# A written issue order in place of a list scheduler, in a kernel of windowed attention and a softplus MLP

## The chip, the core and the metric

One core of a Trainium2 chip runs the whole program. The metric is the device time of one execution in microseconds; the number for a kernel is the median of its runs. Five engines matter here: TensorE (PE, matrix products, with a separate row PEld for its weight loads), VectorE (DVE), ScalarE (ACT), GpSimd (POOL) and SyncE (SP, which here only issues DMA transfers). Each engine executes its own instructions strictly in the order in which the program lists them, and an instruction whose data is not there yet holds up everything behind it on that engine.

## The reference

Inputs are float32: q, k and v of shape (4, 8, 768, 64) and two weight matrices. Four sequences of 768 positions with 8 heads are attended, each row to 8 global keys and to the 96 nearest keys before it (the position itself included), with a bias that falls linearly with distance. The result, 3072 rows of 512, goes through an MLP with a softplus between its two products.

```python
scores = scale * np.matmul(q, k.transpose(0, 1, 3, 2))
is_global = pos[None, :] < int(n_global)          # 8
is_local = (rel >= 0) & (rel < int(n_local))      # 96
dist = np.where(is_global & ~is_local, float(n_local), np.abs(rel))
scores = scores + (-slopes[:, None, None] * dist[None, :, :])[None, :, :, :]
scores = np.where(is_global | is_local, scores, -1e9)
a = softmax(scores)                               # written out in the reference
x = (a @ v) as 3072 x 512
h = x @ w_in                                      # 512 x 2048
g = np.maximum(h, 0.0) + np.log1p(np.exp(-np.abs(h)))
out = g @ w_out                                   # 2048 x 512
```

## The kernel before

**Tiling.** The 3072 rows are 24 blocks of 128 positions. Two blocks of one sequence make a unit (`UNITS`, 12 of them), whose q, k and v are loaded together; blocks 2g and 2g+1 make group g of the MLP (12 groups). A block needs its own keys and those of the block before it, and the 8 global keys, which are copied into rows of the previous block that the window does not reach (`gk`, `gv`). Loads are float32 into a ring of 12 `raw` tiles; DVE, ACT or POOL casts them to bf16 (`cast`). Units 0 to 2 are transposed on PE (`tr`, evicted in two halves by `cp`), the others by DMA transposes on SP.

**Operations and their names.** The program is a list of 987 named operations, each one instruction or a few of one engine. In the order of the data they are:

- `ldq`, `ldk`, `ldv` with a unit's number, `win` and `wout` (eight 512 KB pieces of each weight matrix, line 831): loads, nearly all issued by SP. Units 0 to 2 load q and k in two halves, `.0` and `.1`.
- `castq`, `castk`, `castv` (lines 851 and 875), `cin`, `cout` (line 833): casts to bf16.
- `trq`, `trk` (lines 938 and 958), `cpq`, `cpk` (line 945): transposition of q and k, and its eviction.
- `biasFalse`, `biasTrue` (line 1311 to 1313): the bias of each head for the first block of a sequence and for the others. Blocks 0 and 1 get their bias through PE (`sb`, lines 1000 and 1044).
- `sc` (lines 1010 and 1063): the scores of a block, into the PSUM tiles `s_ps`; `z` (line 1089): DVE adds the bias; `ex` (lines 1023 and 1096): ACT takes the exponential.
- `pv` (line 1115): weights times values for half the heads, with a column of ones for the sum; `nm` (lines 1126 and 1127): DVE divides; `xt`: transposes the block's result, on PE for blocks 0 to 5 (line 1146, evicted by `xc`, line 1151), by DMA on SP for the others (line 1158).
- `a{g}.{p}` (line 1173): eight products with w_in for group g, pair p of 16 slices, into `h_ps[p % 2]`; `e` (line 1188) and `ln` (line 1199): softplus on ACT as ln(1 + exp(h)).
- `b{g}.{ns}.{x}` (line 1222): two or four products with w_out for half of group g; `oc` (line 1251) evicts 128 rows and `st` (line 1254) stores them.
- `fill0` to `fill34` (line 1335): matmuls on a blank tile that nothing reads.

PSUM is held in eight banks: `s_ps` twice two, `x_ps`, two `h_ps`, `o_ps`. Some products of the second layer use `s_ps` and `x_ps` too.

**What sets the order.** `Planner` is a list scheduler that runs while the program is built. Each operation carries the tiles that it reads and writes, an estimated duration and a rank; `due` moves the rank forward from the ranks of its users, plus a correction from the table `NUDGE` (some 280 entries), and `run` simulates the engines, gives each free engine its ready operation of lowest rank, and returns the order in which they started. The table `CHOICE` says on which engine an operation with a choice runs, where it departs from a default. The instructions are then emitted in that order:

```python
    pl.due(last, NUDGE)
    order = pl.run()
    ...
    for o in order:
        o.ins = o.fn()
```

A layer below adds semaphores for all data that crosses engines. DMA transfers take turns over eight semaphores, so that at most eight are in flight. Loads from unit 3 on also wait for a marked `a` operation (`gates`).

Of the kernel before, what the change touches and what calls it, by code (L numbers as in the profile page):

```python
# [16 lines left out]
class Op:  # L17
    __slots__ = (
        "eng", "dur", "lat", "rank", "fn", "deps", "users", "idx", "start", "end", "done",
        "left", "work", "pkt", "ins", "name", "sync", "count", "lane", "port", "alts",  # L20
    )


class Planner:

    LANES = 8
    COLD = 5.7
    FETCH = 18.0  # L30
    FETCH_COST = 1.0
    DMA_FIRST = 0.62
    DMA_LAST = 1.4
    LAT = {"PE": 0.30, "DVE": 0.15, "ACT": 0.21, "POOL": 0.15, "SP": 0.0}

    def __init__(self):
        self.ops = []
        self.writer = {}
        self.readers = {}

    def op(self, name, eng, dur, rank, fn, reads=(), writes=(), after=(), dma=None, sync=(), count=1,
           port=False, alts=None):
        o = Op()
        o.alts = None
        if alts:
            eng = CHOICE.get(name, eng)
            o.alts = [(e, d, e == "POOL" or (e == "DVE" and port)) for e, d in alts.items()]
            dur, port = next((d, p) for e, d, p in o.alts if e == eng)
            inner = fn
            fn = lambda: inner(eng)  # L50
        o.name, o.eng, o.dur, o.rank, o.fn = name, eng, dur, rank, fn
        o.idx = len(self.ops)
        o.lat = self.LAT[eng]
        o.work, o.pkt = dma if dma else (0.0, 0.0)
        o.start = o.end = o.ins = None
        o.sync = list(sync)
        o.count = count
        o.port = port or eng == "POOL"
        deps = set(after) | set(sync)
        for t in reads:  # L60
            if t in self.writer:
                deps.add(self.writer[t])
        for t in writes:
            if t in self.writer:
                deps.add(self.writer[t])
            deps.update(self.readers.get(t, ()))
        for t in reads:
            self.readers.setdefault(t, []).append(o)
        for t in writes:
            self.writer[t] = o  # L70
            self.readers[t] = []
        deps.discard(o)
        o.deps = deps
        self.ops.append(o)
        return o

    def due(self, last, shift, dma=2.4):

        users = {o: [] for o in self.ops}
        for o in self.ops:  # L80
            for d in o.deps:
                users[d].append(o)
        for o in reversed(self.ops):
            t = last(o)
            lag = o.dur + (o.work + dma if o.work else 0.0)
            for u in users[o]:
                t = min(t, u.rank - lag - (0.0 if u.eng == o.eng else o.lat))
            o.rank = t + shift.get(o.name, 0.0)

    def run(self, first=0.7, fixed=None, stretch=None):  # L90
        ops = self.ops
        dma_first, dma_last = self.DMA_FIRST, self.DMA_LAST
        stretch = stretch or (lambda o: 1.0)
        for o in ops:
            o.users = []
            o.done = False
            o.end = None
        for o in ops:
            o.left = len(o.deps)
            for d in o.deps:  # L100
                d.users.append(o)
        engines = ("PE", "DVE", "ACT", "POOL", "SP")
        ready = {e: [] for e in engines}
        free = {e: True for e in engines}
        events, seq = [], 0
        for o in ops:
            if not o.left:
                heapq.heappush(ready[o.eng], (o.rank, o.idx, o))
        now = first
        held = 0.0  # L110
        fetch = self.FETCH
        at = {e: 0 for e in engines}
        moved = [] if fixed is None else sorted((o for o in ops if o.work), key=lambda o: o.lane)
        queues = {"SP": [], "ACT": [], "POOL": []}
        order = []

        def push(t, kind, what):
            nonlocal seq
            seq += 1
            heapq.heappush(events, (t, seq, kind, what))  # L120

        def tell(users):
            for u in users:
                u.left -= 1
                if not u.left:
                    heapq.heappush(ready[u.eng], (u.rank, u.idx, u))

        def rates():
            live = [q for q in queues if queues[q] and queues[q][0][2] <= now + 1e-9]
            total = sum(queues[q][0][0].pkt for q in live)  # L130
            return {q: queues[q][0][0].pkt / total for q in live}

        while True:
            for e in engines:
                if free[e] and ready[e]:
                    if fixed is None:
                        o = ready[e][0][2]
                        if o.work:
                            if len(moved) >= self.LANES and not moved[-self.LANES].done:
                                continue  # L140
                            o.lane = len(moved)
                            moved.append(o)
                        heapq.heappop(ready[e])
                    else:
                        o = fixed[e][at[e]] if at[e] < len(fixed[e]) else None
                        if o is None or o.left:
                            continue
                        if o.work and o.lane >= self.LANES and not moved[o.lane - self.LANES].done:
                            continue
                        at[e] += 1  # L150
                    o.start = now
                    free[e] = False
                    order.append(o)
                    dur = o.dur * stretch(o)
                    if e == "PE" and now < self.COLD:
                        dur *= 2.0
                    if o.port:
                        dur += max(0.0, held - now)
                        held = now + dur
                    push(now + dur, "free", o)  # L160
            r = rates()
            t_dma, q_dma = None, None
            for q in queues:
                if not queues[q]:
                    continue
                if q in r:
                    t = now + queues[q][0][1] / r[q]
                else:
                    t = queues[q][0][2]
                if t_dma is None or t < t_dma:  # L170
                    t_dma, q_dma = t, q
            t_ev = events[0][0] if events else None
            if t_ev is None and t_dma is None:
                break
            t = min(x for x in (t_ev, t_dma) if x is not None)
            for q in r:
                queues[q][0][1] -= (t - now) * r[q]
            now = t
            if now >= fetch and r:
                queues[min(r)][0][1] += self.FETCH_COST  # L180
                fetch = 1e9
            for q in r:
                if queues[q][0][1] <= 1e-7:
                    o = queues[q].pop(0)[0]
                    o.end = now + dma_last
                    push(o.end, "done", o)
            while events and events[0][0] <= now + 1e-9:
                _, _, kind, o = heapq.heappop(events)
                if kind == "free":
                    free[o.eng] = True  # L190
                    if o.work:
                        queues[o.eng].append([o, o.work * stretch(o), now + dma_first + 1.8 * (o.eng == "POOL")])
                    else:
                        o.end = now
                        tell([u for u in o.users if u.eng == o.eng])
                        push(now + o.lat, "done", o)
                else:
                    o.done = True
                    tell([u for u in o.users if o.work or u.eng != o.eng])
        assert all(o.done for o in ops), [o.name for o in ops if not o.done][:20]  # L200
        self.span = max(o.end for o in ops)
        return order

# [61 lines left out]
NUDGE = {  # L265
    "a0.0": -1.75,
    "a0.1": 2,
    "a0.2": 8,
    "a0.3": -34.25,
    "a0.4": -1.25,  # L270
    "a0.5": -23.75,
    "a0.6": 1.75,
    "a1.1": 1,
    "a1.4": -9,
# [366 lines left out]
def kernel(  # L641
# [819 lines left out]
    if globals().get("PLAN_ONLY"):  # L1461
        return
# [42 lines left out]
```

## Time and profile before

| | us |
|---|---|
| median of 3 runs | 218.51 (217.66 to 218.69) |
| profiled execution, first to last instruction | 216.6 |
| PE busy | 208.8 |
| ACT busy | 166.6 |
| DVE busy | 116.0 |
| POOL busy | 78.8 |

The profile is of one execution; its own time is the span of 216.6 us plus what lies around it, and the median of the runs is 1.9 us above that span. It is read from several views. The page has the busy time of each engine and the chain of work that ended last: from the last instruction back, at each step to what released it. The chain can also be listed piece by piece for a stretch of time. The table of stretches gives busy time by engine for stretches of time that one chooses. The list of waits says which engine stood still for whose result. The timeline lists instructions in order of time. Rows give the time from the start, the duration, the engine, the line, the operation and what it writes and reads, as `out<-in`; a number after x counts instructions. Since each operation is a known number of instructions on its engine and each engine keeps its order, every instruction of the trace can be put to its operation by counting, and times of named operations in this text come from that.

### The profile page before, as it was taken

The page shows a single profiled execution, that of the slowest core. Times are in us where ns is not written, and L with a number is a line of the kernel's source. Part 1 is how long each engine was busy: PE and PEld are TensorE (multiplying, and loading weights), DVE is VectorE, ACT ScalarE, POOL GpSimd, SP SyncE. Part 2 cuts the span into 40 slices and gives each one's busy share as a digit, 9 for nine tenths or more (in the row PEclk, how much of TensorE's full clock was granted, in tenths as well). Part 3 has the DMA queues.
Part 4 walks back from the last instruction along what each step waited for, and adds up shares of the span by engine and source line. Part 5 has one row for each costly group of instructions (what it writes and reads, how often), then busy time and mean ns, then how long its engine had stood idle before and what let it go on. Part 6 is the DMA issues. An engine that isn't in the chain of part 4 may idle for free.

```text
span 216.6 us, 4949 instructions
## 1 busy us (share of the span) xinstructions
PE 208.8 (96%) x1974; PEld 142.4 (66%) x2003; DVE 116.0 (54%) x220; ACT 166.6 (77%) x227; POOL 78.8 (36%) x135
## 2 busy tenths in 40 slices
PE   7897999999999999999999999999999999999994
PEld 2455787657665787757767667756766767767554
DVE  7358977956489567337546546346645952101121
ACT  4798999996895699978788688678697878778300
POOL 4636624264159525900265462232237320000000
DMA  6999999999999499945886996892587212011112
GB/s 208 309 391 365 387 358 369 315 240 269 265 278 190 121 221 263 217 104 168 146 222 171 206 164 171 211 156 73 127 222 190 72 25 76 0 51 50 48 48 97
DMA packets 69846, 40.95 MB, mean 189 GB/s; under 512 B 30144, under 2 KB 61248, under 8 KB 69824
## 3 DMA queue, kind: packets, MB, share of 16 engines
q1 hardware_dynamic: 69392, 40.05, 71.1%
q10 hardware_dynamic: 432, 0.59, 0.9%
q8 instruction: 15, 0.25, 0.5%
q14 instruction: 7, 0.06, 0.1%
HBM read 27.26 MB, written 6.29 MB: 155 GB/s over the span
## 4 chain that ended last, share of the span: by engine, by line
PE 86%; DMA 6%; ACT 3%; DVE 2%; issue 1%; SPq 1%; ACTq 0%
PE h_ps L1173 37%; PE o_ps L1222 30%; PE s_ps L1222 6%; PE s_ps L1063 5%; PE x_ps L1115 5%; DMA raw<-in_k_dram 4%; DMA raw<-in_q_dram 2%; PE x_ps L1222 2%; ACT pb L1096 1%; ACT e L1188 1%; SPq L790 1%; PE s_ps L938 1%; ACT g L1199 0%; DVE vb L875 0%; DVE z L1089 0%
## 5 line engine op out<-in xcount | busy, mean ns | idle before, releaser
L1173 PE MATMUL h_ps<-XT,w_in_bf 128*128 128x256 bf16 x768 | 95.6, 273 | 0.2
L1173 PEld LDWEIGHTS <-w_in_bf 128*128 128x128 bf16 x768 | 73.1, 98 | 17.6 <-issue 0.6
L1188 ACT ACTIVATE e<-h_ps 128x512 f32<-128x512 f32 x96 | 60.1, 630 | 22.2 <-PE h_ps L1173 22.0
L1222 PE MATMUL o_ps<-w_out_bf,g 128*128 128x512 bf16 (+1 forms) x295 | 73.6, 371 | 1.2
L1222 PEld LDWEIGHTS <-g 128*128 128x128 bf16 x416 | 37.3, 98 | 28.9
L1089 DVE TENSOR_TENSOR z<-s_ps,biasA 128x1024 f32<-128x1024 f32 x38 | 45.8, 1218 | 15.0 <-PE s_ps L1063 9.2
L1199 ACT ACTIVATE g<-e 128x1024 bf16<-128x1024 f32 x48 | 50.5, 1056 | 1.3
L1096 ACT ACTIVATE pb<-z 128x1024 bf16<-128x1024 f32 (+1 forms) x44 | 43.4, 989 | 9.1 <-DVE z L1089 9.1
L1251 DVE COPY osb<-o_ps 128x512 f32<-128x512 f32 (+1 forms) x20 | 13.4, 671 | 38.2 <-PE o_ps L1222 37.9
L875 POOL CAST vb<-raw 64x512 bf16<-64x512 f32 x38 | 23.3, 614 | 15.7 <-DMA raw<-in_v_dram 14.4
L981 POOL COPY vb<-vb 4x512 bf16<-4x512 bf16 x27 | 16.5, 610 | 33.6 <-PE x_ps L1115 32.1
L875 POOL CAST kb<-raw 64x512 bf16<-64x512 f32 x32 | 19.6, 613 | 22.8 <-DMA raw<-in_k_dram 21.6
L1115 PEld LDWEIGHTS <-pb 128*128 128x128 bf16 x352 | 16.3, 98 | 7.3 <-ACT pb L1096 1.0
L1127 DVE TENSOR_TENSOR xs<-x_ps,rcp 128x256 bf16<-128x256 f32 x40 | 17.0, 424 | 1.6 <-DVE rcp L1126 0.3
L1126 DVE RECIPROCAL rcp<-x_ps 128x4 f32<-128x4 f32 x40 | 7.2, 179 | 17.7 <-PE x_ps L1115 17.3
L1115 PE MATMUL x_ps<-vb,pb 128*128 128x65 bf16 x304 | 15.8, 193 | 0.0
L1222 PE MATMUL s_ps<-w_out_bf,g 128*128 128x512 bf16 (+1 forms) x62 | 13.0, 352 | 0.1
L1335 PE MATMUL x_ps<-blank 128*128 128x512 bf16 x33 | 11.0, 484 | 1.4 <-DVE blank L1274 1.2
L1063 PEld LDWEIGHTS <-kT 64*128 64x128 bf16 x224 | 6.8, 94 | 5.1 <-issue 5.1
L1063 PE MATMUL s_ps<-qT,kT 64*128 64x128 bf16 x224 | 9.9, 218 | 0.1
L1089 DVE TENSOR_TENSOR z<-s_ps,bias 128x512 f32<-128x512 f32 x6 | 3.9, 686 | 7.0 <-PE s_ps L1063 6.9
L1335 PEld LDWEIGHTS <-blank 128*128 128x128 bf16 x35 | 3.7, 117 | 5.9 <-issue 3.3
(82 smaller groups left out, 109.0 us busy)
## 6 DMA issues: line engine op xcount, KB each, us to landing
raw<-in_v_dram SPq DMA_DIRECT2D x12, 512.0 KB, 5.5
out_dram<-osb SPq DMA_DIRECT2D x23, 256.0 KB, 2.3
raw<-in_q_dram SPq DMA_DIRECT2D x9, 512.0 KB, 4.5
raw<-in_k_dram SPq DMA_DIRECT2D x9, 512.0 KB, 4.8
raw<-in_moe_w_in_dram SPq DMA_DIRECT2D x8, 512.0 KB, 9.1
raw<-in_moe_w_out_dram SPq DMA_DIRECT2D x8, 512.0 KB, 8.9
raw<-in_k_dram SPq DMA_DIRECT2D x6, 256.0 KB, 8.2
raw<-in_q_dram SPq DMA_DIRECT2D x4, 256.0 KB, 7.1
```

Source lines behind the costliest of these rows:

```text
L875: copy_on[eng](dst, src)
L981: copy_on[eng](vb_of(prev)[sl, :, 0:D], vb_of(first)[sl, :, 0:D])
L1063: nc.tensor.matmul(reg if unit_of(n) in WIDE else reg.rearrange("p (r t) -> p r t", r=2), kt[rows, 2 * part + m, :], qv(rows, 2 * part + m ...
L1089: nc.vector.tensor_tensor(z, src, bias, ALU.add)
L1096: nc.scalar.activation(pb[:, 0:nr, :].rearrange("p (y a) b -> p y (a b)", y=2), src, AF.Exp, scale=1.0 / root_d)
L1115: nc.tensor.matmul(xv[:, h, :], pb[:, 4 * (h % 2) + 2 * part + h // 2 if lone else u_all * (2 * (h % 2) + h // 2) + u, :], vb_of(prev if u ...
L1127: nc.vector.tensor_tensor(xs[:, 4 * part : 4 * part + 4, :], xv[:, :, 0:D], rcp[:][:, :, None].to_broadcast([P, 4, D]), ALU.mult,)
L1173: last = nc.tensor.matmul(hv[:, j, :], w_in_bf[:, m, fb * P : fb * P + P], XT[g % NXG][:, m, :], start=(m == 0), stop=(m == NM - 1),)
L1188: nc.scalar.activation(e[:, p % 2, :, :].rearrange("p j (b t r) -> p (j b) r t", b=2, r=2), hb[:].rearrange("p (a r t) -> p a r t", a=4, r=2),
L1199: nc.scalar.activation(gt[:, 2 * p - 2 : 2 * p + 2, :].rearrange("p a t -> p (a t)"), e[:].rearrange("p a j t -> p (a j t)"), AF.Ln, bias=1.0,
L1222: nc.tensor.matmul(bank(key)[:, 0 : z - a], gt[:, fb, ns * P : ns * P + P], w_out_bf[:, fb, a:z], start=(fb == 0), stop=(fb == NFB - 1),)
L1335: nc.tensor.matmul(x_ps[:], blank[:, 0:P], blank[:])
```

## The change

The scheduler, its ranks, `NUDGE` and `CHOICE` are gone. `ORDER` is a string that lists all 987 operations with a letter for the engine (P, V, A, G, S for PE, DVE, ACT, POOL, SP), and the instructions are emitted in the order of that list. It was found by a search over whole orders, in which a PSUM tile is read by one engine at a time. The 987 operations and what each computes stay the same; `in_order` asserts that each stands behind what it depends on. 125 operations run on another engine than before: 39 go from POOL to DVE, 29 from POOL to ACT, 25 from DVE to ACT, 14 from DVE to POOL, 10 from ACT to DVE and 8 from ACT to POOL. Many, and all kinds, stand at another place. The diff, with the parts of the list that the text speaks of:

```diff
-class Planner:
-...
+class Program:
+    def __init__(self, placed):
+        self.placed = placed
+        self.ops, self.writer, self.readers = {}, {}, {}
+
     def op(self, name, eng, dur, rank, fn, reads=(), writes=(), after=(), dma=None, sync=(), count=1,
-           port=False, alts=None):
+           port=False, alts=None, mutex=None):
         o = Op()
-...
+        o.name, o.eng, o.fn, o.sync, o.ins = name, eng, fn, list(sync), None
         if alts:
-            eng = CHOICE.get(name, eng)
-...
+            o.eng = self.placed[name]
+            assert o.eng in alts, (name, o.eng)
+            o.fn = lambda: fn(o.eng)
+        assert o.eng == self.placed[name], name
         deps = set(after) | set(sync)
...
+    def in_order(self):
+        done = set()
+        for name in self.placed:
+            o = self.ops[name]
+            assert all(d.name in done for d in o.deps), (name, [d.name for d in o.deps if d.name not in done])
+            done.add(name)
+            yield o
+        assert len(done) == len(self.ops)
+
+ENGINES = {"P": "PE", "V": "DVE", "A": "ACT", "G": "POOL", "S": "SP"}
+ORDER = """
+blank:V table:A ones:G ldk0.0:S ldq0.0:A ident:G fill0:P ldk0.1:S ldq0.1:A fill1:P iota:G fill2:P ldv0:S fill3:P
+ldq1.1:S dl0a:V fill4:P dl1a:V ldk1.0:S dl0b:V fill5:P dl1c:V fill6:P ldk1.1:S dl0c:V fill7:P dl1e:V d0:G fill8:P
+castk0.0:A d0e:V ldv1:S fill9:P biasTrue0:V biasFalse7:A ldq1.0:S biasTrue5:V fill10:P biasTrue4:A biasTrue6:V
+biasFalse3:A fill11:P biasTrue1:A win1:S biasFalse6:V castq0.1:G biasFalse5:A fill12:P win3:S castq0.0:A castk0.1:G
+biasFalse1:A biasTrue3:A trq0.0:P biasFalse4:G biasTrue2:A trk0.0:P win0:S cpq0.0:A biasFalse0:G fill13:P fill14:P
+cpk0.0:A fill15:P win2:S castq1.1:V fill16:P biasFalse2:A fill17:P cpq0.1:V cpk0.1:A fill18:P castk1.0:G win4:S
+sb0.0:P biasTrue7:A castv0.10:V fill19:P castv0.00:G castv0.11:A sc0.0:P castk1.1:V sb1.1:P ex0.0:A sc1.1:P
+castv0.01:G ex0.1:A sb1.0:P sc1.0:P ex1.1:A fill20:P pv0.0:P fill21:P ex1.0:A fill22:P castv1.00:G nm0.0:V trk1.0:P
+fill23:P castq1.0:V pv0.1:P castv1.11:A fill24:P castv1.01:V pv1.1:P win5:S cpk1.0:A fill25:P nm0.1:V win7:S
+trq1.0:P cpk1.1:A cin1:G nm1.1:V win6:S fill26:P fill27:P cpq1.0:A xt0:P pv1.0:P cpq1.1:A fill28:P ldk2.1:S nm1.0:V
+castv1.10:A sc2.0:P ldk2.0:S xc0:A gv4.0:V fill29:P fill30:P z2.0:V xt1:P cin0:G fill31:P xc1:A z2.1:V sc3.0:P
+gv4.1:A fill32:P cin3:G a0.1:P z3.0:V ex2.0:A ex2.1:A pv2.0:P cin2:G a0.0:P ldq2.1:S e0.1:A nm2.0:V ldq2.0:S ex3.0:A
+gk4:G pv2.1:P sc3.1:P nm2.1:V a0.3:P e0.0:A cin4:G wout0:S z3.1:V ln0.0:A xt2:P a0.2:P cin5:G wout2:S e0.3:A xc2:V
+pv3.0:P e0.2:A fill33:P a0.5:P wout1:S cin7:V ex3.1:A nm3.0:V a0.4:P e0.5:A wout3:S cin6:V pv3.1:P fill34:P e0.4:A
+castk2.1:G nm3.1:V ldv2:S a0.7:P ln0.1:A castk2.0:G wout4:S a0.6:P castq2.1:V e0.7:A ln0.2:A xt3:P castq2.0:V
+trk2.0:P xc3:V trq2.0:P e0.6:A a1.1:P cout0:G cpq2.0:V cpk2.0:A cpk2.1:A a1.0:P cpq2.1:V e1.1:A wout5:S cout2:V
+...
+castk3.10:G ln1.2:A b0.0.10:P b0.1.8:P castk3.01:G b0.1.10:P e1.7:A cout7:G trk3:S pv5.1:P ln1.3:A
+...
+e11.4:A ln11.2:A b11.1.4:P b11.1.4.384:P a11.6:P e11.7:A b11.0.4:P e11.6:A ln11.3:A b11.1.8.384:P b10.1.8:P
+b10.1.12:P b11.0.8:P oc10.1.0:V b11.1.12.384:P b11.0.12:P st10.1.0:S oc11.1.384:A st11.1.384:S b11.1.8:P oc11.0.0:A
+b11.1.12:P b11.1.0.256:P st11.0.0:S b11.1.4.256:P oc11.1.0:V b11.1.8.256:P b11.1.12.256:P st11.1.0:S oc11.1.256:A
+st11.1.256:A
+"""
+PLACED = {w.rpartition(":")[0]: ENGINES[w.rpartition(":")[2]] for w in ORDER.split()}
...
-NUDGE = {
-    "a0.0": -1.75,
-...
-CHOICE = {
-    "biasFalse0": "DVE",
-...
-    pl = Planner()
+    pl = Program(PLACED)
...
-            op(f"cp{which}{i}.{r}", engs[r % len(engs)], 0.0, rank + 0.1 * r, ev, reads=held([key]), writes=outs,
+            op(f"cp{which}{i}.{r}", engs[r % len(engs)], 0.0, rank + 0.1 * r, ev, reads=held([key]), writes=outs, mutex=held([key])[0],
...
-    pl.due(last, NUDGE)
-    order = pl.run()
-...
-    for o in order:
+    for o in pl.in_order():
         o.ins = o.fn()
```

In the old order the loads of the head stood on SP as `ldk0.1 ldk0.0 ldq1.1 ldv0 ldq1.0 win0 ldk1.0 win1 win3 ldk1.1 win2 ldv1 win4 win5 win6 win7 ldk2.0 ldk2.1 ldq2.1 ldq2.0 wout1 wout2 wout0 ldv2 wout3 wout4 wout6 wout7 ldq3 ldk3 wout5 ldv3 ldq4 ldk4 trq3 ldv4 trk3`; in the new order the second half of that stretch is `wout0 wout2 wout1 wout3 ldv2 wout4 wout5 ldq3 ldk3 wout6 wout7 ldk4 ldv3 trq3 trk3 ldq4 ldv4`.

More of the change, by code (lines that the diff above doesn't have):

```diff
@@ L17 @@
 class Op:
[L18 to L21, printed above, removed]
[L24 to L39 removed]
+    __slots__ = ("name", "eng", "fn", "deps", "sync", "ins")
+class Program:
+    def __init__(self, placed):
+        self.placed = placed
+        self.ops, self.writer, self.readers = {}, {}, {}
     def op(self, name, eng, dur, rank, fn, reads=(), writes=(), after=(), dma=None, sync=(), count=1,
[L42 removed]
+           port=False, alts=None, mutex=None):
         o = Op()
[L44 removed]
+        o.name, o.eng, o.fn, o.sync, o.ins = name, eng, fn, list(sync), None
         if alts:
[L46 to L58 removed]
+            o.eng = self.placed[name]
+            assert o.eng in alts, (name, o.eng)
+            o.fn = lambda: fn(o.eng)
+        assert o.eng == self.placed[name], name
         deps = set(after) | set(sync)
@@ L90, in run @@
[L90 to L202, printed above, removed]
```

429 lines of the change are left out of this document (59 added, 370 removed).

## The prediction

> **What bounds the kernel now.** The page first: the busy row of each engine and the chain that ended last.
>
> ```profile
> span 216.6 us, 4949 instructions
> PE 208.8 (96%) x1974; PEld 142.4 (66%) x2003; DVE 116.0 (54%) x220; ACT 166.6 (77%) x227; POOL 78.8 (36%) x135
> PE 86%; DMA 6%; ACT 3%; DVE 2%; issue 1%; SPq 1%; ACTq 0%
> ```
>
> TensorE (PE) carries 86% of the chain, so a new order pays only where PE stands still or does nothing useful. The table of stretches says where that is (the stretch, its length, then busy time and instructions of PE, PE's weight loads, DVE, ACT and POOL, the granted clock, the DMA share and GB/s).
>
> ```profile
> 1.16:6.69 5.53, 5.52 (x14) 1.94 (x14) 4.04 (x17) 3.49 (x7) 2.91 (x8) 1.00 0.83 282
> 6.69:30.37 23.68, 21.55 (x253) 15.45 (x254) 15.98 (x34) 21.22 (x36) 12.35 (x17) 1.00 1.06 365
> 150.00:200.00 50.00, 49.65 (x457) 35.00 (x462) 19.68 (x35) 39.88 (x52) 10.41 (x19) 1.00 0.34 91
> 213.70:216.60 2.90, 0.00 (x0) 0.00 (x0) 0.29 (x1) 0.00 (x0) 0.00 (x0) 1.00 0.15 45
> ```
>
> I cut at 30.37 because there `a1.1` begins, the first piece of group 1, and both orders have done exactly the same PE work before it. That head has 2.13 us of idle PE and 21 fillers that compute nothing. From 30.37 to 213.70 the same view gives 181.77 us of PE in 183.33, and the table of waits names no engine and no transfer that PE waits for there: its five PE rows all lie in the head.
>
> ```profile
> PE x_ps L1335 <- DVE blank L1274: 1.2, 1, 1.2
> PE s_ps L1063 <- DVE kTa L945: 0.7, 1, 0.7
> PE h_ps L1010 <- DVE kTa L945: 0.7, 1, 0.7
> PE o_ps L1115 <- ACT pb L1096: 0.4, 1, 0.4
> PE x_ps L1335 <- issue: 0.2, 1, 0.2
> ```
>
> So after 30.37 there is nothing to win and all to lose. The chain inside the head says what holds it:
>
> ```profile
> 6.91 8.91 DMA raw<-in_k_dram
> 15.84 0.67 DVE kb L851
> 18.08 0.69 DVE kTa L945
> 19.13 0.84 DVE vb L875
> 20.00 0.70 DVE z L1089
> 20.79 0.63 ACT pb L1096
> 27.56 1.03 PE h_ps L1173 x8
> ```
>
> Unit 1's keys land at 15.81 and its values at 18.95, because w_in pieces were put between them. VectorE (DVE) can therefore add the first bias to block 2 only at 20.00, ScalarE (ACT) starts `ex2.0` at 20.79 and then runs without a stop until `e0.5` ends at 27.51, and only then comes `a0.7` on PE.
>
> **The head, step by step.** The DMA queue is full from 4 to 50 us (share about 1.06 above), so a load moved forward gains what the loads it passes weigh. Landing to landing in this execution: 0.67 us for a 256 KB half of q or k, 1.75 for v, 1.36 for a w_in or w_out piece; one w_in piece took 2.52.
> - First transposition. The new order has ACT cast the first key half (4.48, step 0.52), then three small and two wide biases (steps 0.21 and 0.32 from their rows, 1.27 together), then `castq0.0` (0.62): 6.89 instead of 6.54 for the last q half. `trq0.0` stands ahead of the seed `sb0.0` now and starts at 6.93; before, it came at 7.41. Thirteen fillers instead of fourteen stand ahead, so PE stops for about 0.3 us.
> - Block 0. Six fillers (0.217 each, from the 1.67 us of the seven at 8.41), the seed, one filler, then `sc0.0` at 10.1 to 10.5 (before 10.73). The bias multiply on POOL has no row of 128 columns; between the 0.29 of its 128 copy and the 0.95 of the 256 multiply it has 2.6 us of room before the seed, so it costs nothing.
> - Unit 1. The new SP order sends all of k1, v1 and q1 before any w_in: v1 lands near 11.3 (5.80 of the fourth half, 1.75, three of 0.67, 1.75; up to 12.4 if a slow piece lies ahead), q1 0.67 later, instead of 18.95 and 9.25. `trq1.0` runs at 14.4 to 14.8 and both ACT evictions behind it (0.48 a step) end at 16.0 to 16.6, so `sc2.0` comes at 16.1 to 16.75 instead of 18.82.
> - Group 0. w_in 0 now lands at 16.4 to 17.6 (the spread is the 1.15 by which one piece was slow) and is cast on POOL (1.04): `a0.1` at 18.0 to 18.7, before 19.16. `ex2.0` starts at 18.2 to 18.8 on ACT, not 20.79. From it to the end of `e0.5` both orders have the same ten ACT operations, which took 6.72: 24.9 to 25.5. The last w_in lands at 24.79, as before, since the same bytes lie ahead of it; its cast moves to DVE (0.68). So `a0.7` can start at 25.5 to 26.3, before 27.27.
> - End of the head. The last load of unit 2, q, lands at 27.50 in both (same bytes ahead). With its DVE cast (0.64), 0.09 of hand-over and the eight transposes `trq2.0` (0.50), `a1.1` cannot come before 28.7. PE's own work gives the same: 6.93 plus 21.55 busy plus one more filler 0.22 is 28.7. Between 28.7 and the old 30.37 I take 29.0, near the floor, because the ACT chain above has 0.5 to 1 us of room. Gain 1.4, bounds 1.7 and 0.
>
> **The body.** It holds the same 271 PE pieces. I took the step from each kind of piece to the next kind from the trace and counted the pairs in both orders: 182.9 us before, 182.8 after (score matmuls stand behind four-product w_out pieces six times instead of nine, where they cost 0.3 more than behind others). I take 0. 125 operations change engine: 68 leave POOL, ACT gets 54 and gives 18. Priced by their rows, ACT rises by 15 us to about 181 (84% of the new span), POOL falls by 25, DVE stays. The cover is PE: the densest stretch, group 3, has 10.0 us of ACT work under 11.0 of PE; in the old order group 0 had 10.5 under 10.7. A store eviction on ACT has no row at 512 columns; between 0.27 (128 columns) and the 0.63 of an exponential of that shape I take 0.6. PE-to-PE round trips after 30 us keep at least 0.3 us: the tightest is `e11.5`, 0.63 plus hand-over under the 1.09 of the two pieces between `a11.5` and `a11.7`. The DMA transposes of x for the second block of a group have 4.8 to 6.6 us from the end of its `pv` to the group's first piece; they need 0.75 for the division and 2.4 from issue to landing (`xt8`: 72.53 to 74.96). SP's queue stays in order: stores now stand between loads, and each waits for its copy. If they held a load by a microsecond, the rooms above take it. Cost 0, bound +1.
>
> **The tail.** Last piece, 128-column copy, 64 KB store, as before: ACT copies (0.27) and issues where DVE (0.29) and SP did. 0, within 0.1.
>
> Sum: 216.6 - 1.4 = 215.2 span. The median of the runs lies 1.9 above this execution's span, so 217.1.
>
> **A rule weighed.** The timeline of the start:
>
> ```profile
> 1.17 6.07 PE L1335 MATMUL x_ps<-blank 128*128 128x512 bf16 x14 [1.17 <-DVE blank L1274]
> 8.41 1.67 PE L1335 MATMUL x_ps<-blank 128*128 128x512 bf16 x7
> ```
>
> Fourteen fillers take 6.07 us (0.43 apart), seven later ones 1.67 (0.217 apart), at a granted clock of 1.00 throughout; PE had not stopped once before it sped up near 7 us. In the new order it stops for 0.3 us just then. The Trainium skill, TensorE: Matmul & The Clock Gate, "What's actually happening", says that half speed ends after one busy window of about 3.4 us and that the windows run free. The trace agrees in that the speed changes once, early. By that rule the stop could cost one more window at half speed, an estimate of 1.7 us by that page.
>
> **Rivals.**
> - Half speed lasts on. If the stop keeps PE at 0.43 us a filler up to the seed, two transpositions of 0.45 and six fillers of 0.217 take twice as long: 2.2 us, of which the stops that the head still has take up some 0.5. PE's own work already binds at 28.7, so `a1.1` comes at 30.4: no gain, 218.5. Against it: 0.3 us is small beside the 5.9 of unbroken work ahead of it. 0.2, in which hand-overs that I set too low end too.
> - Slower: unit 3's transposed keys are late. In POOL's new order `castk3.10` and `castk3.01` stand behind `cout6`, which waits for w_out 6, and SP has two loads and `trq3` ahead of `trk3`. `sc6.0` needs it, and comes at 51.2 (before 55.06, of which 3.5 is its new place). By the queue, `trk3` lands at 52.92 less the two loads it now passes (3.7): 49.2, 2.0 early. But if w_out 6 lands as late as the old last piece (44.14), cast 1.04 and two casts 0.61 end at 46.4; `trq3` held SP 3.35 and `trk3` took 4.7 from issue to landing: 54.5, PE stops 3.3 us, 220.4. It decides once `trk3` lands after 53.7. 0.18.
> - More gain. If no w_in piece is slow by 1.15, all landings move up by that and the floor is 27.6: 216.0. For it: all other pieces take 1.36. Against: PE's own 28.7. 0.08.
> - The order is the old one in writing: excluded, since the operations above move.
>
> **Numbers.** Main case 0.54 with its own range 216.6 to 217.7. A change of 0.5% (1.1 us) is about what a measurement tells, that is 217.4 and 219.6. Part of the main case lies above 217.4: faster 0.53, same 0.29, slower 0.18. The range takes the main case, the larger gain and no gain, and part of the slower case: 215.9 to 219.3.
>
> **What would show it.** Right: `ex2.0` near 18.5, `a1.1` near 29.0, no PE wait after that, ACT near 181 us, and PE ending 183.3 us after `a1.1`, near 212.3. Wrong: PE waits for kT, XT or e between 30 and 200 us; a filler spacing of 0.43 past 8 us; `a1.1` later than 30.

## The result

The new order takes 216.25 us (median of 6 runs, 216.09 to 216.60), the old one 218.53 beside it. The ratio is 0.9905, with a 95% interval of 0.9883 to 0.9928: 2.3 us faster, where 1.4 were forecast. The profiled execution has a span of 214.2 us and a time of 216.13.

The page of the new order, busy rows and shares of the chain that ended last:

```profile
span 214.2 us, 4986 instructions
PE 208.3 (97%) x2003; PEld 142.3 (66%) x2003; DVE 117.9 (55%) x230; ACT 179.1 (84%) x263; POOL 55.4 (26%) x89
PE 90%; DMA 7%; SPq 1%; ACT 1%; POOL 0%; issue 0%
```

ACT does 12.5 us more than before and POOL 23.4 less, and PE carries 90% of the chain instead of 86%. The table of stretches of the new order (stretch, length, busy time and instructions of PE, PE's weight loads, DVE, ACT and POOL, granted clock, DMA share, GB/s), in its own cuts for the head and the body and in two of the old ones:

```profile
1.16:6.69 5.53, 4.46 (x13) 1.58 (x13) 2.53 (x13) 3.42 (x10) 1.82 (x7) 1.00 0.80 262
...
6.69:28.36 21.67, 21.19 (x254) 15.41 (x255) 14.33 (x33) 20.90 (x36) 11.96 (x17) 1.00 1.07 377
28.36:212.30 183.94, 182.65 (x1740) 125.31 (x1737) 100.75 (x183) 154.39 (x219) 40.99 (x62) 1.00 0.70 170
...
150.00:200.00 50.00, 50.00 (x423) 32.89 (x422) 20.39 (x38) 38.77 (x54) 4.77 (x8) 1.00 0.31 78
```

`a1.1`, the end of the head, begins at 28.36 instead of 30.37. PE's waits in the new order, the whole list:

```profile
PE x_ps L933 <- DVE blank L872: 1.2, 1, 1.2
PE s_ps L536 <- POOL qb L449: 1.3, 1, 1.3
PE o_ps L713 <- ACT pb L694: 0.2, 1, 0.2
```

All three are in the head: the first filler, the first transposition and `pv2.0`. The chain of the new order through the head, in order of time (start, duration, what):

```profile
2.06 6.16 DMA raw<-in_v_dram
8.65 8.16 DMA raw<-in_moe_w_in_dram
16.86 1.05 POOL w_in_bf L431
17.91 0.61 ACT vb L579
18.55 0.64 ACT pb L694
...
27.68 0.89 PE s_ps L536 x16
28.58 1.53 PE h_ps L771 x14
```

No key or value of unit 1 is in it any more (the values in its first row are unit 0's). It runs over w_in 0 (landing at 16.81), ACT's `ex2.0` (18.55), and then PE without a gap. The step from the cast of w_in 0 to ACT's copy is the view's inference: ACT's piece before that copy ended at 17.88, so w_in 0 held `ex2.0` by 0.03 us at most. `a0.1`, at 17.95, needs both that cast, which ended at 17.90, and the copy `xc1`, which ended at 17.88. The timeline of the new order at both ends of the head:

```profile
1.17 4.46 PE L933 MATMUL x_ps<-blank 128*128 128x512 bf16 x13 [1.17 <-DVE blank L872]
6.89 0.62 PE L536 MATMUL s_ps<-ident,qb 128*128 128x128 bf16 x8 [1.25 <-POOL qb L449]
...
27.43 0.43 DVE L449 CAST qb<-raw 128x512 bf16<-128x512 f32 x1 [0.17 <-DMA raw<-in_q_dram]
27.97 0.61 PE L536 MATMUL s_ps<-ident,qb 128*128 128x128 bf16 x8
28.41 1.25 PE L771 MATMUL h_ps<-XT,w_in_bf 128*128 128x256 bf16 x10
```

The last cast of unit 2 follows its load (27.41) and ends at 27.86, just before the last transposition. PE has no pause in front of that transposition, though: its weight loads follow those of the one before at an unbroken 0.056 us from each to the next. So `a1.1` came when PE's own stream was through, and the load was in time by some 0.05 us.

**A ledger.** The records of PE's weight loads are complete in both traces (2003), unlike those of its matmuls, so a piece's place can be taken from its weight loads. From the first load of `a1.1` to the last load of the program the new order takes 182.38 us. In it every piece has one fixed price, the step between its matmuls and the next ones in the new order, whose matmul records are complete too: 0.87 for an `a` piece, 0.86 for a four-product w_out piece, 0.66 for 16 score matmuls (0.55, and 0.11 at the border before them), 0.24 for eight `pv`, 0.22 for four transposes of x, whatever stands beside it. What exceeds these prices is a stop, and the new order has none (0.01 us in all). A span is then `a1.1`, plus 182.38, plus stops, plus the rest behind the last weight load. All runs, worked out in this way from their traces (stops is the body less 182.38):

| kernel | median, us | ratio and 95% interval | span | `a1.1` | stops | rest |
|---|---|---|---|---|---|---|
| before | 218.53 | | 216.6 | 30.37 | 0.67 | 3.1 |
| new order | 216.25 | 0.9905 (0.9883 to 0.9928) | 214.2 | 28.36 | 0.00 | 3.5 |
| newhead_oldbody | 221.36 | 1.0139 (1.0107 to 1.0171) | 219.4 | 28.39 | 5.49 | 3.1 |
| newhead_oldbody2 | 217.24 | 0.9979 (0.9949 to 1.0008) | 215.4 | 28.15 | 1.73 | 3.1 |
| oldhead_newbody | 219.50 | 1.0065 (1.0037 to 1.0093) | 217.4 | 30.34 | 1.17 | 3.5 |
| new_oldloads | 226.67 | 1.0372 (1.0339 to 1.0406) | 225.3 | 39.45 | 0.00 | 3.5 |
| old_newloads | 224.57 | 1.0284 (1.0244 to 1.0324) | 222.0 | 35.19 | 1.34 | 3.1 |
| v1_late | 226.27 | 1.0383 (1.0336 to 1.0430) | 224.0 | 38.11 | 0.06 | 3.5 |
| no_late_fill | 217.18 | 0.9947 (0.9920 to 0.9973) | 215.3 | 28.24 | 1.15 | 3.5 |
| no_early_fill | 218.15 | 0.9993 (0.9968 to 1.0017) | 216.9 | 30.96 | 0.12 | 3.5 |
| two_readers | 219.20 | 1.0040 (1.0024 to 1.0056) | 217.3 | 30.42 | 1.02 | 3.5 |
| old_one_reader | 218.21 | 1.0002 (0.9981 to 1.0023) | 215.9 | 29.13 | 1.30 | 3.1 |
| end_sp | 215.81 | 0.9873 (0.9847 to 0.9899) | 213.7 | 28.28 | 0.00 | 3.0 |
| margins | 217.11 | 0.9927 (0.9900 to 0.9955) | 214.5 | 28.24 | 0.44 | 3.5 |

So the 2.33 us of span (216.55 to 214.22) came as 2.01 in the head and 0.67 in the body, less 0.35 behind the last load.

### The profile page after: what moved, and what is told of

Its sections match the earlier page's. It is cut to its first block, busy times and chain, and to the rows that moved or that the text cites. A ratio compares the mean times of both kernels' runs of the same rounds, so it can differ in the third digit from the quotient of the medians.

```text
span 214.2 us, 4986 instructions
## 1 busy us (share of the span) xinstructions
PE 208.3 (97%) x2003; PEld 142.3 (66%) x2003; DVE 117.9 (55%) x230; ACT 179.1 (84%) x263; POOL 55.4 (26%) x89
## 4 chain that ended last, share of the span: by engine, by line
PE 90%; DMA 7%; SPq 1%; ACT 1%; POOL 0%; issue 0%
PE h_ps L771 40%; PE o_ps L820 31%; PE s_ps L820 6%; PE s_ps L661 5%; PE x_ps L713 4%; DMA raw<-in_moe_w_in_dram 4%; DMA raw<-in_v_dram 3%; PE x_ps L820 2%; SPq L388 1%; POOL w_in_bf L431 0%; PE o_ps L713 0%; PE s_ps L536 0%; ACT pb L694 0%; ACT vb L579 0%; PE o_ps L744 0%; PE x_ps L744 0%
## 5 line engine op out<-in xcount | busy, mean ns | idle before, releaser
L820 PE MATMUL o_ps<-w_out_bf,g 128*128 128x512 bf16 (+1 forms) x320 | 76.8, 371 | 0.0
L786 ACT ACTIVATE e<-h_ps 128x512 f32<-128x512 f32 x96 | 59.3, 630 | 15.5 <-PE h_ps L771 14.9
L849 DVE COPY osb<-o_ps 128x512 f32<-128x512 f32 x13 | 9.0, 690 | 24.2 <-PE o_ps L820 24.1
L713 PEld LDWEIGHTS <-pb 128*128 128x128 bf16 x352 | 16.9, 98 | 6.1 <-ACT pb L694 0.5
L473 POOL CAST kb<-raw 64x512 bf16<-64x512 f32 x16 | 10.2, 637 | 38.8 <-DMA raw<-in_k_dram 23.5
L473 POOL CAST vb<-raw 64x512 bf16<-64x512 f32 x23 | 14.9, 646 | 15.5 <-DMA raw<-in_v_dram 13.5
L820 PE MATMUL s_ps<-w_out_bf,g 128*128 128x512 bf16 (+1 forms) x64 | 14.7, 352 | 0.0
L579 POOL COPY vb<-vb 4x512 bf16<-4x512 bf16 x12 | 7.9, 655 | 25.8 <-PE x_ps L713 25.2
L579 ACT COPY vb<-vb 4x512 bf16<-4x512 bf16 x10 | 6.1, 614 | 3.5 <-PE x_ps L713 3.4
L473 DVE CAST vb<-raw 64x512 bf16<-64x512 f32 x16 | 7.6, 474 | 1.1 <-DMA raw<-in_v_dram 0.8
```

The source lines that it names most:

```text
L473: copy_on[eng](dst, src)
L579: copy_on[eng](vb_of(prev)[sl, :, 0:D], vb_of(first)[sl, :, 0:D])
L713: nc.tensor.matmul(xv[:, h, :], pb[:, 4 * (h % 2) + 2 * part + h // 2 if lone else u_all * (2 * (h % 2) + h // 2) + u, :], vb_of(prev if u ...
L786: nc.scalar.activation(e[:, p % 2, :, :].rearrange("p j (b t r) -> p (j b) r t", b=2, r=2), hb[:].rearrange("p (a r t) -> p a r t", a=4, r=2),
L820: nc.tensor.matmul(bank(key)[:, 0 : z - a], gt[:, fb, ns * P : ns * P + P], w_out_bf[:, fb, a:z], start=(fb == 0), stop=(fb == NFB - 1),)
```

## The experiments

Each ratio is to runs of the old order beside it (medians 218.1 to 218.5).

**Head alone, body alone.** On every engine the new list up to `a1.1` and then the old one, and the other way round.

```diff
 # each engine's list
-new up to a1.1, new behind it
+new up to a1.1, old behind it      (newhead_oldbody)
+old up to a1.1, new behind it      (oldhead_newbody)
```

> The new order up to a1.1 on every engine, then the old order for all that is left, with the old choice of engines there. Theory (the head carries the gain, 2.0 of 2.4 us in the two traces): a1.1 near 28.4, time 2.0 us under the old kernel, 0.1 to 0.4 above the new one. Rival (the body's own order and its engines carry much of it, 0.66 in the traces, or the head's gain is lost again in the old body): 1.3 us or less under the old kernel.

> The old order up to a1.1, then the new one. Theory: a1.1 near 30.4, time 0.2 to 0.7 us under the old kernel (body 0.66 shorter, tail 0.3 longer). Rival: the new body needs what the new head did earlier, and PE waits in it: no gain or slower.

With the new head, `a1.1` comes at 28.39, so the gain of 2.0 is made there. But the kernel is 3 us slower than the old one. Its PE waits, DVE in the timeline, and the granted clock behind the stop (the number before the last two):

```profile
PE s_ps L659 <- DVE qT L541: 3.0, 1, 3.0
```

```profile
31.36 0.69 DVE L429 CAST w_out_bf<-raw 128x1024 bf16<-128x1024 f32 x1 [2.50 <-DMA raw<-in_moe_w_out_dram]
31.97 1.28 DVE L541 COPY qT<-s_ps 128x512 bf16<-128x512 bf16 x2
```

```profile
32.00:34.00 2.00, 0.69 (x18) 0.57 (x18) 1.85 (x4) 0.10 (x1) 0.00 (x0) 1.00 1.10 356
34.00:36.00 2.00, 2.00 (x13) 1.49 (x12) 1.96 (x2) 0.66 (x2) 1.31 (x2) 0.59 1.05 384
36.00:38.00 2.00, 1.78 (x9) 1.17 (x9) 1.15 (x3) 2.00 (x4) 0.34 (x1) 0.55 1.13 329
```

The old list of DVE casts w_out 1 ahead of unit 2's queries, because the old SP order sent that piece first; the new SP order sends it third. DVE stands 2.5 us for it, `sc4.0` waits 3.0 behind that, and the clock then falls to 0.59 and 0.55 for 4 us, some 1.7 us of work. That is the seam and not a property of either half. With the old head before the new body the seam is smaller: `a1.0` waits 0.9 for `e0.6`, since the new ACT list has `ln0.2` ahead of it, and the rival is right that the new body builds on what the new head did earlier. Behind `a2.0` it runs like the new order.

**The head with the seam mended.** As newhead_oldbody, but SP goes over to the old list already at its first w_out piece.

```diff
 # SP
-wout0 wout2 wout1 wout3 ldv2 wout4 wout5
+wout1 wout2 wout0 ldv2 wout3 wout4 wout6
```

> As the first splice, but of SP's list only the first 20 loads are the new ones; from the first w_out piece on SP keeps the old order, so that the w_out piece that the old DVE list casts ahead of the unit 2 evictions lands as early as it did. Theory (the head gives 2.0 us; the first splice lost it at its seam, where DVE stood behind that cast): a1.1 near 28.4, sc4.0 without a stop of 3 us, 1.7 to 2.2 us under the old kernel. Rival (the old body cannot use an earlier start): less than 1 us under the old kernel.

The 3 us stop is gone, which confirms the seam. `a1.1` comes 2.2 us earlier than in the old order, yet at the end 1.2 of span and, by the runs, 0.2% are left, with an interval that includes no gain. The 1.7 to 2.2 us that I expected did not come; the rival's less than 1 us did. The old body stops again (the first three rows of its waits inside the body):

```profile
PE s_ps L659 <- DVE qT L541: 0.4, 1, 0.4
PE s_ps L659 <- POOL kT L567: 0.3, 1, 0.3
PE s_ps L659 <- ACT qT L541: 0.3, 1, 0.3
```

By the ledger it has 1.73 us of stops where the old order had 0.67: the old body gives back half of an earlier head.

**The loads alone.** Only the first 20 loads on SP change places.

```diff
 # SP, the first 20 (old_newloads; new_oldloads is the reverse)
-ldk0.1 ldk0.0 ldq1.1 ldv0 ldq1.0 win0 ldk1.0 win1 win3 ldk1.1 win2 ldv1 win4 win5 win6 win7 ...
+ldk0.0 ldk0.1 ldv0 ldq1.1 ldk1.0 ldk1.1 ldv1 ldq1.0 win1 win3 win0 win2 win4 win5 win7 win6 ...
```

> The new kernel with only the first 20 loads on SP put back in their old order (unit 1's k, v and q between the w_in pieces). Theory (the load order opens the head): v of unit 1 lands near 19 again, ex2.0 starts near 21, a1.1 near 30.4 or later, time 2 us or more above the new kernel. Rival (the engine choices and the order of the instructions do it, and the loads are early enough either way): within 0.5 us of the new kernel.

> The old order with only the first 20 loads on SP in their new order. Theory: the loads alone bring nothing, because DVE has the cast of w_in 0 ahead of the first division and would wait for that piece until about 17 us: 1 to 4 us slower than the old kernel. Rival: the earlier v and k of unit 1 are worth their 2 us by themselves: about 1 to 2 us faster than the old kernel.

Both signs as expected, both sizes larger: the new order loses 10.4 us with the old loads, the old order 6.1 with the new ones. In old_newloads DVE stands before w_in 0, which now lands at 16.43, while the division of block 0, `nm0.0`, waits behind that cast:

```profile
DVE w_in_bf L429 <- DMA raw<-in_moe_w_in_dram: 4.7, 1, 4.7
```

In new_oldloads the same happens on POOL (4.7 us for v1) and DVE (5.1 for a key). Then a small copy on DVE, `gv4.0`, takes 4.82 us where it took 0.28 in the new order (more on it under v1 alone), and PE's clock falls, as the table of stretches of new_oldloads shows:

```profile
20.00:22.00 2.00, 0.95 (x19) 0.70 (x17) 1.89 (x4) 2.00 (x5) 2.00 (x3) 1.00 1.01 379
22.00:24.00 2.00, 1.22 (x7) 0.57 (x5) 2.00 (x1) 1.38 (x3) 2.00 (x4) 0.50 1.03 377
...
30.00:32.00 2.00, 2.00 (x20) 1.35 (x18) 0.75 (x4) 1.59 (x3) 1.04 (x1) 0.50 1.00 386
32.00:34.00 2.00, 2.00 (x21) 1.78 (x20) 1.90 (x4) 1.52 (x2) 1.04 (x1) 0.94 0.21 79
```

From 22 to 32 us it is 0.50, and PE is busy for 6.89 of these 10 us. So of the 11.1 us by which the head is longer some 3.4 are clock, an estimate as half of 6.89, and the others waits. Loads and lists belong together.

**v1 alone.** The new order with one load moved.

```diff
 # SP
-ldk1.1 ldv1 ldq1.0 win1 win3 win0 win2 win4
+ldk1.1 ldq1.0 win1 win3 win0 win2 ldv1 win4
```

> The new order with one load moved on SP: v of unit 1 goes behind the fourth w_in piece, as late as in the old order. Its values are first needed by pv2.0 (19.2 in the new kernel). Theory (what counts is the place of the cast in a list that cannot pass it: POOL casts v of unit 1 ahead of w_in 1 and 0): v lands near 19, a0.1 not before 22, 3 to 6 us above the new kernel. Rival (only the use counts): 0 to 0.7 us above the new kernel.

One misplaced load costs 10 us, more than expected. POOL's first cast of v1 stands ahead of w_in 1 and w_in 0 in its list and waits 6.6 us. DVE's and ACT's casts of it wait 4.4 and 4.7, and PE stops for 3.7 us, since the division `nm0.1` stands behind DVE's. `sc2.0` comes at 19.9 (16.0). Then POOL casts w_in pieces almost without a pause, and DVE does nothing but one copy, 4 rows by 512 (the first row is of the new order, the others of v1_late):

```profile
16.43 0.28 DVE L579 COPY vb<-vb 4x512 bf16<-4x512 bf16 x1
...
18.81 3.99 POOL L429 CAST w_in_bf<-raw 128x1024 bf16<-128x1024 f32 x4
20.24 4.84 DVE L577 COPY vb<-vb 4x512 bf16<-4x512 bf16 x1
22.91 2.02 POOL L429 CAST w_in_bf<-raw 128x1024 bf16<-128x1024 f32 x2
```

The copy, `gv4.0`, ends 0.15 us behind POOL's last cast of that run, and in new_oldloads, where it takes 4.82 us, too; no other copy of global keys or values on DVE took more than 1.2 us in any trace. That POOL's casts hold it is argued from this; no run moved one. The bias of block 2, `z2.0`, stands behind it and begins at 25.0 (16.63), `a0.1` comes at 26.3 (17.95), and the clock is 0.50 to 0.53 from 20 to 30 us here too. That v1's landing held the head is confirmed; its price is not the delay alone, as I took it, but also the run of casts that the delay pushes together, and the clock.

**The fillers.** Without the 22 behind the first transposition, and without the 13 before it.

```diff
-FILLERS = 35
+FILLERS = 13      (no_late_fill; no_early_fill keeps the other 22)
```

> The new order without the 22 fillers that stand behind the first transposition. Theory: from a0.1 on only two of them lie in a full PE stream, and there the cast of the last w_in piece (25.4) holds a0.7 anyway, so 0 to 0.3 us faster than the new kernel. Rival (the fillers keep PE at full speed through the stops of the head): half speed comes back between 8 and 18 us and the time is 0.5 us or more above the new kernel.

> The new order without the 13 fillers ahead of the first transposition, so that PE's first work is that transposition near 6.9. Theory (PE starts at half speed, 0.43 us a filler, and needs some us of work to leave it): the transpositions and the fillers behind them take twice as long, a1.1 0.5 to 2 us later, time 0.5 to 2 us above the new kernel. Rival (the stops of the head hide it, or the speed does not hang on the work before): within 0.4 us of the new kernel.

Without the late ones the head is as fast (`a1.1` at 28.24, full clock), but 0.9 us are lost in all: the size is the rival's, the half speed that it named is not in this trace. That 22 fillers less, 4.8 us of PE work, bring `a1.1` only 0.11 forward fits the load of unit 2 standing right behind PE's own stream. The trace shows two stops in the body, 0.53 at `a4.1` and 0.62 at `a6.0`; the first in its timeline (the row counts 0.46 of it as idle):

```profile
81.06 1.05 PE L768 MATMUL h_ps<-XT,w_in_bf 128*128 128x256 bf16 x8 [0.46 <-DMA XT<-xs]
```

`xt9` was issued at 74.97 and landed at 81.01; in the new order it was issued at 74.99 and landed at 79.23, 1.4 us before its use. But this transfer also took 4.9 to 5.7 us in the traces of end_sp, two_readers and no_early_fill, which have the late fillers, against 4.24 in the new order and 6.04 here. That the missing fillers made it late is therefore not shown. Without the early fillers half speed lasts longer, as the timeline of no_early_fill shows (fillers 0.43 apart past 8 us):

```profile
6.93 1.04 PE L533 MATMUL s_ps<-ident,qb 128*128 128x128 bf16 x8 [6.93 <-POOL qb L446]
8.61 2.77 PE L930 MATMUL x_ps<-blank 128*128 128x512 bf16 x6
```

`a1.1` then comes 2.6 us later than in the new order, beyond the 0.5 to 2 that I gave, and the time is 1.9 longer, within it.

**One reader to a PSUM tile.** The new order with three evictions of keys put back on DVE, and the old order with the same three on ACT.

```diff
 # two_readers, ACT
-cpq0.0 cpk0.0 biasFalse2 cpk0.1
+cpq0.0 biasFalse2 cpk0.1
-castv1.11 cpk1.0 cpk1.1
+castv1.11 cpk1.1
-cpk2.0 cpk2.1
+cpk2.0
 # two_readers, DVE
-cpq0.1 castv0.10
+cpq0.1 cpk0.0 castv0.10
-castv1.01 nm0.1
+castv1.01 cpk1.0 nm0.1
-xc3 cpq2.0
+xc3 cpk2.1 cpq2.0
 # old_one_reader: the three go from DVE to ACT
+cpk0.1 cpk0.0
+cpk1.1 cpk1.0
+cpk2.1 cpk2.0
```

> The new order, with one part undone: three evictions of transposed keys in the head (cpk0.0, cpk1.0, cpk2.1) go back from ACT to DVE, so that ACT and DVE each read one half of the same PSUM tile, as before the change. Theory: the second reader waits for the first (in the old trace DVE waited 1.6 us in two such places), and the scores sc0.0 and sc2.0 come 0.3 to 0.7 us later; but a0.1 waits for w_in 0 and a1.1 for the last load of unit 2, so only a part of that is left at a1.1: 216.2 to 216.7 us. Rival: the two halves are read side by side and ACT, which never rests here, is relieved of about 1.5 us: sc2.0 0.5 earlier, the time 0 to 0.3 below the new order.

> The old order with one part of the change: the second halves of the transposed keys of units 0, 1 and 2 (cpk0.0, cpk1.0, cpk2.1) are read by ACT, right beside the other half, instead of by DVE. Putting them back on DVE in the new order cost 3 us. Theory: in the old order the same saving is hidden, because sc2.0 may come 0.3 us earlier (18.5) but DVE adds the bias only at 20.0, after the cast of v1, which lands at 18.95; a1.1 stays at 30.2 to 30.6 and the time within 0.3 us of the old order, 218.2 to 218.7. Rival: one reader to a tile is worth its 2 to 3 us in any order; then a1.1 comes near 28.4 and the time is 216 to 217 us.

In the new order this part is worth 3 us, more than the whole change gained and far more than I expected. ACT's waits and its timeline in two_readers:

```profile
ACT kTa L541 <- DVE kTa L541: 3.0, 2, 1.9
```

```profile
8.13 0.31 ACT L907 ACTIVATE bias<-dist 128x128 bf16<-128x128 f32 x1
10.39 0.59 ACT L541 COPY kTa<-s_ps 128x512 bf16<-128x512 bf16 x1 [1.94 <-DVE kTa L541]
```

The second copy carries a wait for the first, so ACT, which has no rest in the head, stands until DVE has got through the cast and the copy ahead of it. `sc0.0` comes at 11.0 (9.9), `sc2.0` at 17.8 (16.0), `a1.1` at 30.42, and `sc4.0` waits 0.9 more for DVE's queries behind the third such pair. The two halves share the source tile and the destination tile; which of the two the wait is for was not tried apart. Nor was any other of the 125 changes of engine tried by itself. In the old order the same three edits change nothing that the runs can tell (1.0002). There DVE still stands before v1, which landed at 18.3 in that trace:

```profile
18.32 0.42 DVE L471 CAST vb<-raw 64x512 bf16<-64x512 f32 x1 [1.05 <-DMA raw<-in_v_dram]
```

Its `a1.1` at 29.13 was earlier than I expected (v1 landed 0.65 earlier in that trace), but the body gave 0.63 of it back in stops. So neither the loads nor the readers bring the gain by themselves.

**The last store, and margins.** The store of the last 128 columns on SP's queue instead of ACT's; and beside that, no late fillers and two transposes earlier on SP.

```diff
-            on, queue = ("ACT", "ACT") if c == 1 else ("DVE", "SP")
+            on, queue = ("ACT", "SP") if c == 1 else ("DVE", "SP")
 # margins only: FILLERS = 13, and SP
-ldq6 ldk6 xt8 xt9
+xt8 ldq6 ldk6 xt9
-st4.0.0 st3.1.0 xt13
+xt13 st4.0.0 st3.1.0
```

> The new order, with one change: the store of the last 128 columns is issued by SP instead of ACT's queue. ACT still copies them out of PSUM. Theory: the tail gave back 0.3 to 0.4 us because the program ends 1.27 us after the last store lands when ACT's queue carries it, and 0.86 us after it when SP's does. Expected: the same head and body (a1.1 at 28.4, PE ending at 212.3 within 0.1), the span 0.3 to 0.4 shorter, 215.8 to 216.0 us. Rival: what follows the last store does not depend on the queue that issued it; then nothing changes, 216.2.

> The new order with four edits: the 22 fillers behind the first transposition are left out, the last store is issued by SP, and two DMA transposes of x on SP's queue move ahead of what stood before them (xt8 ahead of the loads ldq6 and ldk6, xt13 ahead of the stores st4.0.0 and st3.1.0). Theory: without the late fillers the loss was 0.53 us at a4.1 and 0.62 us at a6.0, where PE waited for transposes that landed 1.6 to 1.8 us later than in the new order's trace. With xt8 issued about 3 us earlier, xt9 lands about 0.5 earlier, xt13 about 1.4 earlier, and both waits go. Then a1.1 at 28.2, 182.4 us of unbroken PE work and the shorter tail give 215.5 to 215.8 us. Rival: the late landings come from elsewhere and stay: 216.5 to 217 us, with PE waits for XT at a4 or a6.

end_sp is the fastest kernel of the study, 215.81 us and a span of 213.7. Its interval and that of the new order overlap, but its span is 0.5 shorter, 0.1 in the head and 0.4 behind the last store: that landed at 212.83, and the program ended 0.88 later, against 1.29 in the new order. Still, the reason that I gave is not shown: in margins the same store goes out on SP's queue, lands at 213.23, and the program ends 1.30 later all the same. In both slow endings a gap of some 0.4 us lies on SP, behind its wait for the store; what makes it stays open.

margins missed its 215.5 to 215.8. The transposes did as expected: `xt9` landed at 80.58, 0.43 earlier than in no_late_fill, and `xt13` at 109.95, 1.87 earlier; the stop at `a4.1` shrank to 0.1 and that at `a6.0` went. But `a4.0` came 0.35 late behind a `pv` that waited for POOL, and the tail stayed long. In 4 of its 7 runs the mean granted clock was 0.991 or 0.992, and those took 217.1 to 218.1, the other three 216.0 to 217.0. In no_late_fill 5 of 12 had 0.992. With the late fillers (the new order, end_sp, two_readers) none of 24 was under 0.998, and none of the 12 of no_early_fill under 0.997. So these fillers seem to keep the clock up in some executions, which no single profile showed. What that is worth is open: in no_late_fill the executions of both kinds took the same (medians 217.14 with the lower clock, 217.22 without).

## Why the prediction was right, and what in it was wrong

**Head: 1.4 forecast, 2.01 measured.** The mechanism held. v1 landed at 12.07 (11.3 to 12.4 forecast), w_in 0 at 16.81 (16.4 to 17.6), `ex2.0` began at 18.55 (18.2 to 18.8), `e0.5` ended at 25.28 (24.9 to 25.5). `sc0.0` at 9.94, `sc2.0` at 15.97, `a0.1` at 17.95 and `a0.7` at 25.48 were up to 0.2 ahead of their bounds. Mis-sized were both floors of 28.7 and what I put on them. The floor that held is PE's own work: PE was busy 21.19 us between 6.69 and `a1.1`, not 21.77, and stood still for 0.48: 28.36. Why the same work has less busy time is open. The floor of the load was too high as well and lies just under it: the DVE cast took 0.43 instead of the 0.64 of the old row, the load landed 0.09 earlier, and `a1.1` began 0.45 behind the start of the transposition, not 0.50. I added 0.3 for waits, and that `a1.1` stood behind both floors at once was right.

**First transposition: right time, wrong reason.** It began at 6.89 (6.93 forecast), but held by POOL's cast of the second q half, which landed at 6.17 (5.13 before), not by ACT. PE stopped for 1.25 us, not 0.3, since the 13 fillers ended sooner: from one to the next they are 0.43 apart up to 4.13 us and 0.22 behind it, where the old order's were 0.43 apart to the last. The speed did not fall back, so the half-speed rival did not come about in this order. Its price was real: no_early_fill shows half speed up to about 11 us and `a1.1` at 30.96, later than the rival's 30.4.

**Body: 0 forecast, 0.67 gained.** "After 30.37 there is nothing to win and all to lose" is the step that failed. The old body had 0.60 us of stops in five places of 0.04 to 0.20 (`a1.0`, `b0.0.8` behind `pv5.0`, `pv8.0`, `a4.4`, `a9.2`), and the list of PE's waits names none of them. The waits of PE's weight loads between 30.4 and 213 us show two of them, in the old order:

```profile
PEld L1063 <- issue: 6.8, 20, 0.4
PEld L1173 <- issue: 0.4, 2, 0.2
```

and none at an `a` piece in the new order (28.4 to 213 us):

```profile
PEld L661 <- issue: 5.7, 17, 0.4
```

At `a9.2`, the second of PE's eight weight loads starts at 163.59, 0.31 behind the first, just as ACT's exponential `e9.0` on the same bank ends at 163.54; that ACT held the bank is argued from this, not shown. Of the other four stops the cause is open. My pair prices were also wrong: score matmuls cost 0.66 behind any piece. The 0.3 that they seemed to cost more behind w_out pieces is where the trace sets the border between two pieces. ACT came to 179.1 (181 forecast) and covered its extra work as I said.

**XT's room: right that it held, wrong by how much.** I set 3.2 us as needed, 2.4 of them from issue to landing. `xt9` took 4.24 from issue to landing and `xt13` 4.35, which left 1.4 and 0.6 us. no_late_fill shows how little that is.

**Tail: 0 within 0.1 forecast, 0.35 lost** behind the last weight load. From the landing of the last store to the end it is 1.29 us instead of 0.86, as told under end_sp.

**Slower rival.** `trk3` landed at 48.62 (49.2 forecast), 1.9 before `sc6.0` at 50.54: refuted here. But its kind, a queue that stands for one load while what others need lies behind it, is just what made newhead_oldbody, both load swaps and v1_late slow.

**More gain.** The time came near this rival's 216.0, but not for its reason: one w_in piece was slow again (w_in 2 landed 2.48 us behind the piece before it); here it came behind w_in 0 and so did not delay it.

The sum: 2.01 + 0.67 - 0.35 = 2.33 of span, where 1.4 stood. That the total is no further off owes something to luck, since the body's gain and the tail's loss, neither of them forecast, have opposite signs; 216.25 is below the main case's own range. The profiled time lies 1.9 above the span, as taken.

## What to carry to other kernels

Before calling a busy engine dense, price each piece from records that are complete and look for what exceeds the price: half a microsecond was hidden in five stops that the list of PE's waits did not name. A load order and the order of the casts on in-order engines are one thing; changing the loads alone cost 6 to 10 us here, because one cast waited with others behind it, and because the casts that it held then came in one run. Look at the duration of small operations in such a run too: a copy of 0.28 us that took 4.8 stands in no list of waits. What an order gains early is kept only if the rest can follow: the old body gave back half of the same head.

## What was not expected of the hardware

The granted clock went back to 0.50 without one long silence: in new_oldloads PE was busy 0.77 of the 2 us from 18 and 0.95 of the 2 from 20, with no stop above 1.23 us, and then ran at half speed for 10 us, with a stop of 3.11 in them and busy at full length in the last four. In v1_late one silence of 3.73 us stood before the fall. The Trainium skill, TensorE: Matmul & The Clock Gate, "What's actually happening", gives at least one idle window of about 3.4 us as the condition. v1_late agrees; in new_oldloads no stretch of 3.4 us before the fall was idle throughout, and in the last one, from 18.6 to 22.0, PE was busy for 1.22 us. How busy such a stretch may be was not tried. A stop of 1.25 us, in the new order, cost no clock. At the very start the column of the granted clock reads 1.00 while fillers run 0.43 apart, so there it does not show the half speed.

A small copy on DVE can take as long as POOL's casts beside it: 4.84 and 4.82 us for `gv4.0` in v1_late and new_oldloads, 0.28 in the new order.

Fillers that only seemed to fill stops may have a use: their absence showed in the mean clock of 9 of 19 executions and in none of 24 with them. They are no guard against a longer stop: with them, behind a stop of 3.0 us, all four executions of newhead_oldbody had a mean of 0.991 or 0.992.
